# Splitting a 256-query block of the second layer's attention into two blocks of 128

## Chip, cores and metric

The kernel runs on one NeuronCore of a Trainium2 chip. The metric is the device time in microseconds; a median is over the runs named. Before the change: 971.18 us, median of 3 runs (968.93 to 971.66).

## The reference

Two layers, each an attention block and an MLP block, on one sequence of 2048 tokens of width 448. The same weights serve both layers.

```python
x = A_x
for _ in range(2):
    x = x + A(layernorm(x), A_wqkv, A_wo)   # 16 heads of 28, softmax over 2048 keys
    x = x + B(layernorm(x), w1, b1, w2, b2) # relu(x w1 + b1)^2 w2 + b2, F = 1792
```

## The kernel before

Rows are cut into 16 row tiles of 128, numbered 0 to 15. `blocks` says how many tiles form one query block of the attention, for each layer. For every block and every group of four heads (`g`), score matmuls fill a PSUM tile of three banks, one exponential (ScalarE) turns it into bf16, and value matmuls accumulate 28 outputs and one denominator for each head. When all four groups of a block are normalised, the block's **chain** starts: output projection, residual add, layernorm, first MLP product (w1), relu and square, second product (w2), residual add, store.

```python
blocks = [[(0, 4), (4, 4), (8, 4), (12, 4)],
          [(0, 4), (4, 4), (8, 2), (10, 2), (12, 2), (14, 1), (15, 1)]]   # (first tile, tiles)
```

A planner written in the kernel emits the instructions. Each stream is a Python generator with a priority; the planner repeatedly takes the step that can start first by its own table of durations, and PE steps of all streams but the scores are admitted only where, by that table, they delay the next scores or the next exponential by 0.6 us at most. The engines then execute this fixed order, each in its own order.

```python
    pl.spawn(9.5, heat())            # filler matmuls where PE would be too idle
    pl.spawn(0, s_stream())          # scores
    pl.spawn(1, e_stream())          # exponentials
    pl.spawn(2, p_stream())          # values
    ...
            # in norm_stream, once the 4 head groups of a block are normalised:
            pl.spawn(4 + 0.1 * qb, chain(l, qb))
```

```python
    def norm_stream(l, qb, g, res, oe):
        ...
        tail = qb == len(blocks[l]) - 1
        if tail:                     # last block of a layer: denominators by a matmul, no DMA
            def den(e):
                box["t"] = bank(d, "den")
                nc.tensor.matmul(box["t"][:, 0:n], lhsT=sel[:, :], rhs=res["t"][:, 0:n], start=True, stop=True)
            d = Op("PE", 0.1 + n * 4 / 2400, den, deps=[oe], acq=R_m)
            yield d
            ...                      # reciprocal on VectorE
        else:                        # other blocks: three small DMAs around a small reciprocal
            ...

    def chain(l, qb):
        t0, nt = blocks[l][qb]
        ...
        for j in range(nt):
            a = yield from mm_tile(
                [(0, D, [(oTn[:, g, j * P:(j + 1) * P], wo[:, g, :]) for g in range(G)])],
                add_to_x(t0 + j), 0.62, [*norm_done[l, qb], *[("wo", i) for i in range(G)]])
            yield stats(mv, t0, j, [a])
        ...
        xnT, own_xt, ends = yield from layernorm(t0, nt, None, mv=mv)
        own_h = Op("DVE", 0.0, None, acq=R_h)     # one set of 14 h buffers
        yield own_h
        ...                          # w1, relu, square, w2, residual add, store
```

The PSUM banks are dealt out as 2 x 3 for scores, one for the value accumulator, one (`R_m`) for everything else. Once the last scores are planned, the score banks are open to the chains too, and ScalarE takes the relus.

The softmax here doesn't subtract the row's maximum and nothing guards it: scores larger than these inputs give would overflow.

Of the kernel before, what the change touches and what calls it, by code (L numbers as in the profile page):

```python
# [141 lines left out]
def kernel(  # L142
# [18 lines left out]
    NFC = F // P  # L161
    scale = float(DH) ** -0.5

    blocks = [[(0, 4), (4, 4), (8, 4), (12, 4)], [(0, 4), (4, 4), (8, 2), (10, 2), (12, 2), (14, 1), (15, 1)]]

    x_view = A_x[0].rearrange("(tb p) d -> p tb d", p=P)
    out_view = out[0].rearrange("(tb p) d -> p tb d", p=P)
# [37 lines left out]
    part = [[part_sb[:, g, :] for g in range(G)], [k0_f32[:, g * QB:(g + 1) * QB] for g in range(G)]]  # L205
# [360 lines left out]
    def p_stream():  # L566


        where = {}
        for gi, us in enumerate(groups):  # L570
            for k, (pi, kb, r, hh) in enumerate(us):
                where.setdefault((pi, kb), []).append((gi, k, hh))
        steps = list(where.items())
        last_use = {}
        for si, (_, parts) in enumerate(steps):
            for gi, _, _ in parts:
                last_use[gi] = si
        for si, ((pi, kb), parts) in enumerate(steps):
            l, qb, g, kbs, first, last = passes[pi]
            r = 4 // blocks[l][qb][1]  # L580
            n = blocks[l][qb][1] * P
            opens = kb == kbs[0]
            closes = kb + r - 1 == kbs[-1]
            if opens:
                box = {}

            def fn(e, kb=kb, parts=parts, box=box, opens=opens, l=l, g=g, kbs=kbs, r=r, n=n):
                if opens:
                    box["t"] = ps_o.tile([P, QB], DT.float32, name="oT")
                for i in range(r):  # L590
                    for gi, k, hh in parts:
                        c0 = k * 512 + i * n
                        nc.tensor.matmul(box["t"][DHP * hh:DHP * hh + DHP, 0:n],  # L593
                                         lhsT=V_sb[l][:, kb + i, 4 * g + hh, :],
                                         rhs=gbuf[gi]["pt"][:, c0:c0 + n],
                                         start=(kb + i == kbs[0]), stop=(kb + i == kbs[-1]),
                                         tile_position=(0, DHP * hh))
            gis = sorted({p[0] for p in parts})
            o = Op("PE", 0.23 + 0.01 * r, fn,
                   deps=[("e", gis[-1]), *{("V", l, kb + i) for i in range(r)}],  # L600
                   acq=R_o if opens else None,
                   rel=[gbuf[gi]["e"] for gi in gis if last_use[gi] == si], mode="col")
            if opens:
                opened = o
            yield o
            if closes:
                res = {}

                def ev(e, box=box, first=first, last=last, g=g, res=res, n=n, pt=part[qb % 2][g]):
                    src = box["t"][:, 0:n]  # L610
                    if last:
                        dst = res["t"] = np_.tile([P, QB], DT.float32, name="oT_sb")
                        dst = dst[:, 0:n]
                    else:
                        dst = pt
                    if first:
                        nc.vector.tensor_copy(out=dst, in_=src)  # L617
                    else:
                        nc.vector.tensor_tensor(out=dst, in0=src, in1=pt, op=ALU.add)
                oe = Op("DVE", 0.15 + n / 930, ev, deps=[o], rel=opened, acq=R_os if last else None)  # L620
                yield oe
                if last:
                    pl.spawn(3, norm_stream(l, qb, g, res, oe))
# [185 lines left out]
```

## Time and profile before

| | before |
|---|---|
| profiled span | 970.5 us |
| ScalarE busy | 96% |
| last exponential starts | 941.8 us |
| from that start to the end of the span | 28.7 us |

The kernel has two parts that are read differently. Until about 943 us it is a train of 683 exponentials. After it, work that hangs together step by step runs on engines that are mostly idle. In the profiles PE is TensorE, ACT ScalarE and DVE VectorE; PEclk is the clock granted to PE, as a share of full speed. Of the tiles, sc and mt are PSUM banks, den holds denominators, rec their reciprocals, tp transposes, x_sb the residual stream; L417 is the line of the chain's matmuls. The table by 40 slices of the span (24 us each) of the kernel before shows both parts, in tenths busy and tenths of clock:

```profile
ACT  5999999999999999999989999999999999999982
PEclk9999999999999999999979999999999999999998
```

The reader sees ScalarE full from the second slice to the 38th, but for slice 21, and two places where PE's granted clock dips: slices 21 (the boundary of the layers) and 40 (the tail).

### The profile page before, as it was taken

Reading aid. Unit: us, or ns where it says so; the run is one execution under the profiler, and the core shown is the slowest. Engines: PE = TensorE matmul, PEld = TensorE weight load, DVE = VectorE, ACT = ScalarE, POOL = GpSimd, SP = SyncE. Lnnn points to the kernel's source line nnn. Section 1 sums busy time; section 2 is a strip of 40 time slices with the busy share of each in tenths; the row PEclk is TensorE's granted clock in tenths of the full one; section 3 lists DMA queues with packets and bytes.
Section 4 is the critical chain, followed back from the end, with each engine's and each line's share of the span. In section 5 each row is a group of like instructions: output and inputs, shape, how many; then the busy total and the mean of one; then the engine's idle time right before and its main releaser. Section 6 shows DMA issues by size and latency. Waiting matters only on the chain.

```text
span 970.5 us, 18234 instructions
## 1 busy us (share of the span) xinstructions
PE 868.7 (90%) x7764; PEld 318.5 (33%) x7764; DVE 429.5 (44%) x989; ACT 929.9 (96%) x701; POOL 7.5 (1%) x16
## 2 busy tenths in 40 slices
PE   8888899899989998888988999898999899989886
PEld 3233223233222332222323233223233333434555
DVE  7843325434354344553335433325525533343535
ACT  5999999999999999999989999999999999999982
POOL 3000000000000000000000000000000000000000
PEclk9999999999999999999979999999999999999998
DMA  9000010000000000000000000010000000000000
GB/s 272 4 1 1 2 36 12 11 12 13 12 12 4 11 12 13 1 1 1 1 1 1 1 1 1 12 35 24 12 22 20 10 17 27 13 17 23 12 11 14
DMA packets 23005, 17.17 MB, mean 18 GB/s; under 512 B 10634, under 2 KB 19915, under 8 KB 22924
## 3 DMA queue, kind: packets, MB, share of 16 engines
q1 hardware_dynamic: 22924, 16.02, 5.6%
q8 instruction: 60, 0.98, 0.4%
q14 instruction: 21, 0.17, 0.1%
HBM read 13.73 MB, written 2.06 MB: 16 GB/s over the span
## 4 chain that ended last, share of the span: by engine, by line
ACT 64%; issue 17%; PE 14%; DVE 4%; DMA 0%; ACTq 0%
ACT pt L558 64%; PE mt L417 6%; PE sc L543 3%; PE oT L593 3%; PE sc L417 2%; DVE r L719 1%; PE mt L763 1%; DVE rec L641 1%; DVE x_sb L690 0%; DVE st L310 0%; DMA x_sb<-in_A_x_dram 0%; DVE Q_sb L433 0%; DVE xnT L369 0%; PE tp L359 0%; PE den L635 0%
## 5 line engine op out<-in xcount | busy, mean ns | idle before, releaser
L558 ACT ACTIVATE pt<-sc 128x1536 bf16<-128x1536 f32 (+1 forms) x683 | 918.6, 1713 | 10.4 <-PE sc L543 10.1
L543 PE MATMUL sc<-Q_sb,K_sb 32*128 32x512 bf16 (+2 forms) x2816 | 270.0, 324 | 46.7 <-ACT pt L558 38.3
L593 PE MATMUL oT<-pt,V_sb 128*32 128x512 bf16 (+2 forms) x2816 | 206.7, 331 | 0.1
L543 PEld LDWEIGHTS <-K_sb 32*128 32x128 bf16 x2816 | 93.5, 91 | 300.0 <-issue 289.2
L417 PE MATMUL mt<-xnT,w 128*128 128x512 bf16 (+2 forms) x544 | 122.5, 340 | 16.5 <-DVE r L719 11.1
L719 DVE TENSOR_SCALAR r<-mt 128x512 bf16<-128x512 f32 x105 | 72.5, 691 | 129.0 <-PE mt L417 128.8
L417 PE MATMUL mt<-w,h 128*128 128x448 bf16 x420 | 100.3, 357 | 3.0 <-DVE rec L641 1.3
L690 DVE TENSOR_TENSOR x_sb<-x_sb,mt 128x448 bf16<-128x448 bf16 x61 | 37.8, 620 | 132.0 <-PE mt L417 131.4
L593 PEld LDWEIGHTS <-V_sb 128*32 128x32 bf16 x2816 | 58.6, 94 | 113.9 <-issue 110.6
L763 PE MATMUL mt<-xn,ident 128*128 128x448 bf16 x218 | 73.2, 354 | 12.9 <-DVE r L719 2.2
L417 PEld LDWEIGHTS <-w 128*128 128x128 bf16 x616 | 49.6, 101 | 61.0 <-issue 47.0
L417 PEld LDWEIGHTS <-h 128*128 128x128 bf16 x448 | 35.7, 97 | 47.9 <-issue 27.2
L726 DVE TENSOR_TENSOR h<-r 128x512 bf16<-128x512 bf16 (+1 forms) x113 | 47.5, 421 | 7.1 <-ACT r L717 3.9
L417 PE MATMUL mt<-xnT,wq 128*128 128x512 bf16 x124 | 36.5, 381 | 6.0 <-DVE Q_sb L433 3.8
L310 DVE BATCH_NORM_STATS2 st<-x_sb 128x6 f32<-128x448 bf16 x64 | 39.7, 621 | 2.2 <-DMA x_sb<-in_A_x_dram 0.7
L433 DVE CAST Q_sb<-mt 128x512 bf16<-128x512 f32 x30 | 20.7, 689 | 37.3 <-PE mt L417 37.2
L433 DVE CAST K_sb<-mt 128x512 bf16<-128x512 f32 x29 | 20.0, 691 | 36.9 <-PE mt L417 36.9
L459 DVE CAST V_sb<-mt 128x448 bf16<-128x448 f32 x31 | 19.2, 621 | 35.9 <-PE mt L417 35.9
L417 PE MATMUL mt<-xnT,wk 128*128 128x512 bf16 x116 | 31.7, 388 | 2.6 <-DVE K_sb L433 0.9
L417 PE MATMUL mt<-wv,xnT 128*128 128x448 bf16 x124 | 31.4, 375 | 2.7 <-DVE V_sb L459 2.1
L417 PE MATMUL mt<-wo,oTn 128*128 128x448 bf16 x124 | 30.5, 354 | 3.1 <-DVE x_sb L690 1.5
L617 DVE COPY oT_sb<-oT 128x512 f32<-128x512 f32 (+2 forms) x34 | 17.0, 500 | 35.2 <-PE oT L593 34.9
(75 smaller groups left out, 332.7 us busy)
## 6 DMA issues: line engine op xcount, KB each, us to landing
rec<-scr SPq DMA_DIRECT2D x20, 256.0 KB
x_sb<-in_A_x_dram SPq DMA_DIRECT2D x8, 224.0 KB
out_dram<-x_sb SPq DMA_DIRECT2D x16, 112.0 KB
w<-in_B_w_dram SPq DMA_DIRECT2D x1, 1568.0 KB
rec<-scr SPq DMA_DIRECT2D x12, 128.0 KB
w<-in_B_w_dram SPq DMA_DIRECT2D x1, 1344.0 KB
part_sb<-in_A_wqkv_dram SPq DMA_DIRECT2D x1, 672.0 KB
wo<-in_A_wo_dram SPq DMA_DIRECT2D x4, 98.0 KB
```

The source lines that it names most:

```text
L310: nc.vector.bn_stats(out=st[:, :], in_=x_sb[:, t0 + j, :])
L417: nc.tensor.matmul(box["t"][:, c0:c0 + n], lhsT=lhsT, rhs=rhs, start=a, stop=b)
L433: nc.vector.tensor_copy(out=dst, in_=src)
L459: nc.vector.tensor_copy(out=o, in_=i)
L543: nc.tensor.matmul(sc[:, c0:c0 + nt * P], lhsT=K_sb[l][rows, g, (kb + i) * P:(kb + i + 1) * P], rhs=Q_sb[rows, g, t0 * P:(t0 + nt) * P], s ...
L558: nc.scalar.activation(out=pt[:, 0:n], in_=gbuf[gi]["sc"][:, 0:n], func=AF.Exp, scale=scale)
L593: nc.tensor.matmul(box["t"][DHP * hh:DHP * hh + DHP, 0:n], lhsT=V_sb[l][:, kb + i, 4 * g + hh, :], rhs=gbuf[gi]["pt"][:, c0:c0 + n], start ...
L617: nc.vector.tensor_copy(out=dst, in_=src)
L690: nc.vector.tensor_tensor(out=x_sb[:, tb, :], in0=x_sb[:, tb, :], in1=t[:, 0:D], op=ALU.add)
L719: nc.vector.tensor_scalar(out=r[:, 0:w], in0=t[:, 0:w], scalar1=0.0, scalar2=None, op0=ALU.max)
L726: nc.vector.tensor_tensor(out=h[:, 0:w], in0=r[:, 0:w], in1=r[:, 0:w], op=ALU.mult)
L763: nc.tensor.matmul(t[:, 0:D], lhsT=ident[:, :], rhs=xns[0][:, 0:D], start=True, stop=True)
```

## The change

Intent: with tiles 12 and 13 apart, tile 12's chain can start while tile 13's attention still runs, so less chain work should be left at the end.

```diff
-    blocks = [..., [(0, 4), (4, 4), (8, 2), (10, 2), (12, 2), (14, 1), (15, 1)]]
+    blocks = [..., [(0, 4), (4, 4), (8, 2), (10, 2), (12, 1), (13, 1), (14, 1), (15, 1)]]
...
-    def ev(e, ..., pt=part[qb % 2][g]):
+    def ev(e, ..., pt=part[qb % 2][g][:, 0:n]):
```

More of the change, by code (lines that the diff above doesn't have):

```diff
@@ L162 @@
     scale = float(DH) ** -0.5
-    blocks = [[(0, 4), (4, 4), (8, 4), (12, 4)], [(0, 4), (4, 4), (8, 2), (10, 2), (12, 2), (14, 1), (15, 1)]]
+    blocks = [[(0, 4), (4, 4), (8, 4), (12, 4)], [(0, 4), (4, 4), (8, 2), (10, 2), (12, 1), (13, 1), (14, 1), (15, 1)]]
     x_view = A_x[0].rearrange("(tb p) d -> p tb d", p=P)
@@ L607, in p_stream, with ev @@
                 res = {}
-                def ev(e, box=box, first=first, last=last, g=g, res=res, n=n, pt=part[qb % 2][g]):
+                def ev(e, box=box, first=first, last=last, g=g, res=res, n=n, pt=part[qb % 2][g][:, 0:n]):
                     src = box["t"][:, 0:n]
```

## The prediction

> **What bounds the kernel now.** I read the busy table first, then the costliest groups, then the starts of the exponentials stretch by stretch, and last the chain of work that ends the run and the timeline of its last 30 us. The page names the leading engine and the line that loads it:
>
> ```profile
> PE 868.7 (90%) x7764; PEld 318.5 (33%) x7764; DVE 429.5 (44%) x989; ACT 929.9 (96%) x701; POOL 7.5 (1%) x16
> ...
> L558 ACT ACTIVATE pt<-sc 128x1536 bf16<-128x1536 f32 (+1 forms) x683 | 918.6, 1713 | 10.4 <-PE sc L543 10.1
> ```
>
> The 683 softmax exponentials fill ScalarE, which waits only 10.4 us before them in the whole run. PE's 90% is softer: it includes 218 filler matmuls (L763), and PE itself waits 38.3 us for an exponential to free a score buffer. So the attention ends when the last exponential ends, and a block split matters only through the pace of the exponentials, or through what remains afterwards. The pace, from the line of the exponential in three stretches (min/median/max ns, first and last start):
>
> ```profile
> L558 ACT ACTIVATE pt<-sc x45: 1485/1752/1872, 829.1 to 888.0; 128x1536 bf16<-128x1536 f32 x45
> ...
> L558 ACT ACTIVATE pt<-sc x21: 1515/1609/1708, 886.6 to 913.5; 128x1536 bf16<-128x1536 f32 x21
> ...
> L558 ACT ACTIVATE pt<-sc x22: 1182/1758/1849, 913.5 to 941.8; 128x1536 bf16<-128x1536 f32 x21, 128x1024 bf16<-128x1024 f32 x1
> ```
>
> The first stretch is nearly all of block (12, 2), 256 queries wide: 58.9 us over 44 steps, 1.339 us each. The other two are blocks (14, 1) and (15, 1), 128 wide: 26.9/20 = 1.345 and 28.3/21 = 1.348 us. The pitch hardly depends on the width. (Durations exceed the pitch because neighbours overlap.)
>
> The last exponential starts at 941.8 and lasts 1.18, so it ends at 943.0; the span ends at 970.5. These 27.5 us are the tail. The chain of work in it, cut to its long pieces (start, us, what):
>
> ```profile
> 941.63 3.01 PE mt L417 x15
> ...
> 945.34 0.93 PE mt L417 x4
> 946.29 0.63 DVE x_sb L690
> ...
> 952.06 0.59 ACT xnT L367
> 952.69 1.86 PE mt L417 x16
> 954.56 3.04 PE sc L417 x32
> ...
> 958.28 3.00 PE sc L417 x15
> 961.28 0.89 PE mt L417 x16
> ...
> 964.41 2.85 PE sc L417 x15
> 967.28 0.62 DVE x_sb L690
> ```
>
> Read against the order of instructions, this is: the second MLP product (w2) of row tile 13; then the output projection of row tile 14, its layernorm, and its MLP; then the MLP of row tile 15. Two MLPs and a layernorm of about 6 us, nearly bare, stand after the attention. Tile 14's attention was done at about 914, 27 us before the end, but its chain had not even begun: each block's chain takes the one set of h buffers, and the chain of tiles 12 and 13 held it to the end.
>
> [...] the chain's sixteen in 0.89 us are 55.6 ns each, so halving the width costs PE little. [...] the table of 2 us windows (window, length, busy time of PE, weight loads, VectorE, ScalarE, GpSimd, granted clock, DMA):
>
> ```profile
> 950.00:952.00 2.00, 0.96 (x5) 0.62 (x6) 1.52 (x8) 0.00 (x0) 0.00 (x0) 0.56 0.00 0
> 952.00:954.00 2.00, 1.33 (x14) 1.30 (x13) 1.76 (x8) 0.58 (x1) 0.00 (x0) 0.50 0.03 8
> 954.00:956.00 2.00, 2.00 (x22) 2.00 (x20) 1.76 (x10) 0.60 (x1) 0.00 (x0) 0.50 0.00 0
> 956.00:958.00 2.00, 2.00 (x30) 2.00 (x28) 0.50 (x2) 0.96 (x2) 0.00 (x0) 0.73 0.00 0
> ```
>
> A mean of 0.56 means half speed for 1.76 of 2 us, 0.73 for 1.08; with the two full rows 6.84 us[...], after the sparse PE work of 946 to 950.
>
> **The change, part by part.** The edit of the list splits block (12, 2) into (12, 1) and (13, 1). The sliced `part` changes nothing: that view is used only for partial sums, and only blocks of 512 have them.
>
> *Attention of tiles 12 and 13.* The number of exponentials stays 683. Score and value matmuls go from 256 each of 256 columns to 512 each of 128, as the order of instructions shows (128-wide score matmuls 512 to 1024). In the timeline, scores for one exponential cost PE 0.39 us as 6 x 256 and 0.40 us as 12 x 128; one value step 0.40 us as 8 x 256 and 0.41 as 16 x 128. Over some 43 exponentials this is 43 x 0.02 = 0.9 us of PE time, under an engine that is not the bound; the planner also drops 14 fillers (218 to 204). Effect on the end: about 0.
>
> *First MLP product, tiles 12 and 13.* 56 matmuls of 256 columns become 112 of 128: 56 x 0.11 = 6.2 us against 112 x 0.056 = 6.3. Hidden.
>
> *VectorE and DMA.* Four more head groups are copied, inverted and multiplied: 8 x (0.29 + 0.17 + 0.28) - 4 x (0.42 + 0.20 + 0.42) = 1.8 us; one more rsqrt chain of 12 small instructions, about 2.3 us; 12 more small DMAs. VectorE is busy 43% there (11.61 of 27 us). Hidden.
>
> *The tail, where the change acts.* Tile 12's chain can now start one 29 us block earlier. The order of the changed kernel, counted in exponentials, has tile 12's MLP done at 665 of 682, tile 13's w1 at 668 to 676, tile 14's projection already at 677, and 12 of the 15 matmuls of tile 13's w2 before the last scores. After those there remain 3 matmuls of tile 13, then tile 14's transposes and MLP, and all of tile 15's chain. So the projection and layernorm of 14 are hidden, but its MLP is not: the planner still places it after the denominators of tile 15. I lay that order out with the old durations, last exponential ending at 943.0:
>
> - value matmuls end at 943.6 (0.2 wait, 14 of the 32 that took 0.63); copy of the last head group to 943.95; two denominator matmuls end at 944.5.
> - VectorE inverts and multiplies twice: from 944.1, 2 x (0.95 + 0.28) plus gaps, to 946.7. Meanwhile tile 14 is transposed.
> - the last projection matmul and the wait put tile 15's residual add at 947.35 (before: 951.63, 0.65 after the multiply).
> - add to start of normalise took 951.63 to 955.69, 4.06; two h squarings of tile 14 (0.42 each) now stand before it: start 952.25, end 952.65. Tile 14's w1 (56 x 0.056 = 3.1 us plus two fillers) fits between 946.8 and 950.6.
> - tile 15's transposes stand before tile 14's w2 on PE, so w2 starts at 953.0; from w2's start to the next w1 was 958.28 to 961.12, 2.84: 955.85.
> - w1 to the final add was 961.12 to 967.28, 6.16: 962.0. From the add to the end of the span 3.2: 965.2.
>
> That is 5.3 us less than 970.5. [...] Net gain 4.7 us: 971.18 - 4.7 = 966.5.
>
> **Rivals.**
>
> 1. *More matmuls slow the exponentials.* PE gets 512 more matmuls and as many weight loads in 57 us. Against: the blocks of tiles 14 and 15 have this very density and ran at 1.345 and 1.348 us with ScalarE busy 100%. For: their gaps were partly free of chain work, and tile 13's w2 now comes in bursts of six near the end (over 1 us in one interval). A loss of 0.05 us a step would be 2 us: about 968.5.
> 2. *The backlog simply moves.* Two MLPs still lie in the tail, as before. If tile 14's transposes or its w1 wait for something not in my order, such as a late reciprocal DMA or a held PSUM bank, only tile 13's removed w2 matmuls count (12 x 0.19 = 2.3 us): about 969.
> 3. *Tile 14 wholly hidden.* The split's full promise: tile 15 alone after the attention, about 962. The order speaks against it; there are still eight relu steps on ScalarE behind the last exponential.
> 4. [...]
>
> **Range and chances.** The three times before spread over 2.7 us (968.93 to 971.66), and the middle of the run has its own half-clock stretches (489 to 500) whose position may vary. Rivals 1, 2 and 4 push up by 2 to 3 us, rival 3 down by 4. So 966.5, with 963.0 to 970.0 for eight in ten. Two per cent is 19 us, nearly the whole tail, and ScalarE's pitch is untouched: within 2% is nearly sure.
>
> **What would show it.** Right: the last exponential still starts at 941 to 943, pitch 1.34 to 1.35 in all of 829 to 942; four fifths of tile 13's w2 and the projection of 14 before it; from its end to the end of the span about 22 us instead of 27.5; one add of tile 15 near 947 and its layernorm, not tile 14's, as the bare stretch before 953. Wrong: ScalarE idle or a longer pitch after 829 (rival 1); w1 of tile 14 starting later than 949 (rival 2); a granted clock of 0.5 after 953 (rival 4); a tail below 20 us (rival 3).

The sum was 5.3 us for the tail, less 0.6 set aside for the clock, which makes 4.7. The fourth rival, half clock over the final two MLPs, put the time at 968 to 969; it is the "rival 4" named further down.

## The result, and the profile after

Ratios are the mean time of one kernel's fast runs over that of the other's in the same rounds, so they are not quite the ratio of the medians quoted. No run of this document differs from the kernel before by 2%; only the intervals tell them apart.

The changed kernel took 967.09 us (median of 6, 964.36 to 968.28) against 969.35 for the kernel before (6 runs): ratio 0.9971, 95% interval 0.9952 to 0.9991. A repetition gave 965.75 against 969.05, ratio 0.9963 (0.9943 to 0.9984). So the gain is about 3.2 us (the mean of 0.29% and 0.37% of 969), with intervals from 0.9 to 5.5 us, where 4.7 was predicted and 963.0 to 970.0 was the range.

The profiled span fell by much more, from 970.5 to 962.6. That is the first thing to clear up. The busy table and two stretches of the exponential in the changed kernel:

```profile
PE 854.3 (89%) x8267; PEld 327.7 (34%) x8318; DVE 433.4 (45%) x1016; ACT 929.2 (97%) x701; POOL 7.5 (1%) x16
```

```profile
L558 ACT ACTIVATE pt<-sc x45: 1515/1610/1840, 828.2 to 887.2; 128x1536 bf16<-128x1536 f32 x45
...
L558 ACT ACTIVATE pt<-sc x19: 1144/1532/1887, 912.5 to 937.8; 128x1536 bf16<-128x1536 f32 x18, 128x1024 bf16<-128x1024 f32 x1
```

In the first stretch, which the change made 128 wide, the pitch is (887.2 - 828.2)/44 = 1.341 us, against 1.339 before: twice as many matmuls do not slow the exponentials. But the last exponential starts at 937.8 instead of 941.8. Those 4.0 us are not the change's, since they arise before it takes effect at about 825 us: at the 601st exponential (826.91 against 831.74) the changed kernel is already 4.8 us ahead, and from there to the last one it loses 0.9 us. Two stretches around the boundary of the layers show it (columns: stretch, its length, busy us of PE, weight loads, VectorE, ScalarE, GpSimd with counts, granted clock, DMA). The kernel before, first profile:

```profile
440.00:465.00 25.00, 22.36 (x149) 6.96 (x147) 7.79 (x10) 24.02 (x19) 0.00 (x0) 0.93 0.01 1
485.00:520.00 35.00, 31.12 (x189) 9.62 (x187) 12.64 (x16) 31.96 (x25) 0.00 (x0) 0.85 0.00 1
```

The kernel before again, a later profile of the same program:

```profile
440.00:465.00 25.00, 22.37 (x158) 7.25 (x157) 8.06 (x11) 25.00 (x20) 0.00 (x0) 1.00 0.01 1
485.00:520.00 35.00, 30.22 (x208) 9.57 (x208) 15.26 (x21) 34.23 (x26) 0.00 (x0) 0.95 0.00 1
```

In the first, ScalarE stood idle for 0.98 + 3.04 = 4.0 us of these stretches, with PE's mean clock at 0.93 and 0.85; in the second for 0.8 us, at 1.00 and 0.95, and there the last exponential starts at 938.2. The changed kernel's profile happened to be of the second kind (25.00 and 34.22). So two profiles of this kernel are to be compared only after the last exponential:

| profile | last exponential starts | span | from that start to the end |
|---|---|---|---|
| before | 941.8 | 970.5 | 28.7 |
| before, again | 938.2 | 966.9 | 28.7 |
| after | 937.8 | 962.6 | 24.8 |
| after, again | 937.8 | 962.7 | 24.8 |

(The last column, here and below, is taken from the times before rounding.) The tail is 3.9 us shorter, and it repeats to 0.1 us. What took it down, and what was worse than predicted, is in the chain of work of the changed kernel (start, us, what):

```profile
939.43 0.43 PE den L635 x2
...
942.44 0.58 PE tp L359 x4
943.02 3.20 PE sc L417 x20
946.22 0.75 PE mt L763 x2
946.97 1.60 PE sc L417 x16
...
950.41 2.84 PE mt L417 x15
953.25 1.79 PE sc L417 x32
```

Tile 13's w2 and tile 14's projection and layernorm, which stood in this chain before, are gone from it. What follows the last denominators is tile 14's transposes (tp), four projection matmuls of tile 15 with sixteen of w1 (x20), then w2 of tile 14 (x15, on the tile "mt") and w1 of tile 15. But the twenty took 3.20 us; at a clock of 1.00 four such projection matmuls took 0.77 us (*warm2*, its chain below) and sixteen of w1 0.89 (kernel before, at 961.28). Here the granted clock was 0.50 (the kernel before has a stretch of half clock in its tail too, 6.8 us long in both profiles, mostly over w1 of tile 14):

```profile
942.00:944.00 2.00, 1.56 (x8) 0.88 (x8) 0.68 (x2) 0.59 (x1) 0.00 (x0) 0.50 0.00 0
944.00:946.00 2.00, 2.00 (x18) 1.77 (x17) 1.38 (x3) 0.00 (x0) 0.00 (x0) 0.50 0.00 0
946.00:948.00 2.00, 2.00 (x17) 1.55 (x15) 1.63 (x11) 0.60 (x1) 0.00 (x0) 0.50 0.00 0
```

One more loss lies in the attention, where the timeline of the changed kernel has

```profile
917.96 1.89 PE L417 MATMUL mt<-xnT,w 128*128 128x128 bf16 x16
```

```profile
920.50 18.48 ACT L558 ACTIVATE pt<-sc 128x1536 bf16<-128x1536 f32 x14 [0.73 <-PE sc L543]
```

The sixteen matmuls ran at a granted clock of 0.50 (918 to 920; in the same trace sixteen took 1.05 to 1.07 us at 897, 900, 903, 922 and 925) and made the next scores late, and ScalarE stood idle for 0.73 us. The kernel before has no wait of ScalarE for scores between 600 us and its last exponential in either profile. Counted by exponentials, from the 601st to the last, the changed kernel loses 0.87 us against either profile of the kernel before (0.80 in its repetition). So the profiles give -3.9 + 0.9 = -3.0 us, which agrees with the measured 3.2; with intervals of 4 us, so close an agreement is luck.

### The profile page after: what moved, and what is told of

Read it like the earlier page. It is cut to its first block, busy times and chain, and to the rows that moved or that the text cites. A ratio compares the mean times of both kernels' runs of the same rounds, so it can differ in the third digit from the quotient of the medians.

```text
span 962.6 us, 19338 instructions
## 1 busy us (share of the span) xinstructions
PE 854.3 (89%) x8267; PEld 327.7 (34%) x8318; DVE 433.4 (45%) x1016; ACT 929.2 (97%) x701; POOL 7.5 (1%) x16
## 3 DMA queue, kind: packets, MB, share of 16 engines
q8 instruction: 65, 1.06, 0.5%
## 4 chain that ended last, share of the span: by engine, by line
ACT 68%; issue 18%; PE 12%; DVE 1%; ACTq 0%
ACT pt L558 68%; PE mt L417 4%; PE sc L543 3%; PE oT L593 2%; PE sc L417 1%; PE oT L233 1%; PE mt L763 1%; DVE r L719 1%; PE tp L359 0%; DVE xnT L369 0%; DVE rec L641 0%; DVE x_sb L690 0%; PE den L635 0%; ACT r L717 0%; ACT Q_sb L431 0%
## 5 line engine op out<-in xcount | busy, mean ns | idle before, releaser
L543 PEld LDWEIGHTS <-K_sb 32*128 32x128 bf16 x3072 | 98.3, 91 | 298.9 <-issue 287.3
L417 PE MATMUL mt<-xnT,w 128*128 128x512 bf16 (+2 forms) x565 | 116.6, 321 | 16.7 <-DVE r L719 10.7
L417 PE MATMUL mt<-w,h 128*128 128x448 bf16 x434 | 102.9, 355 | 2.5 <-DVE x_sb L690 1.0
L593 PEld LDWEIGHTS <-V_sb 128*32 128x32 bf16 x3072 | 62.6, 94 | 110.2 <-issue 103.9
L763 PE MATMUL mt<-xn,ident 128*128 128x448 bf16 x204 | 68.0, 356 | 9.9 <-DVE xnT L369 1.5
L417 PEld LDWEIGHTS <-h 128*128 128x128 bf16 x448 | 35.2, 97 | 45.4 <-issue 23.9
L726 DVE TENSOR_TENSOR h<-r 128x512 bf16<-128x512 bf16 x114 | 47.5, 418 | 5.6 <-ACT r L717 2.5
L417 PE MATMUL mt<-xnT,wq 128*128 128x512 bf16 x115 | 34.5, 380 | 7.2 <-DVE Q_sb L433 4.1
L417 PE MATMUL mt<-xnT,wk 128*128 128x512 bf16 x103 | 30.2, 381 | 3.4 <-DVE K_sb L433 0.9
L369 DVE COPY xnT<-tp 128x1024 bf16<-128x1024 bf16 (+1 forms) x31 | 20.8, 672 | 27.2 <-PE tp L359 27.2
```

The source lines that it names most:

```text
L369: nc.vector.tensor_copy(out=dst, in_=tp[:, :, 0:w])
L417: nc.tensor.matmul(box["t"][:, c0:c0 + n], lhsT=lhsT, rhs=rhs, start=a, stop=b)
L543: nc.tensor.matmul(sc[:, c0:c0 + nt * P], lhsT=K_sb[l][rows, g, (kb + i) * P:(kb + i + 1) * P], rhs=Q_sb[rows, g, t0 * P:(t0 + nt) * P], s ...
L593: nc.tensor.matmul(box["t"][DHP * hh:DHP * hh + DHP, 0:n], lhsT=V_sb[l][:, kb + i, 4 * g + hh, :], rhs=gbuf[gi]["pt"][:, c0:c0 + n], start ...
L726: nc.vector.tensor_tensor(out=h[:, 0:w], in0=r[:, 0:w], in1=r[:, 0:w], op=ALU.mult)
L763: nc.tensor.matmul(t[:, 0:D], lhsT=ident[:, :], rhs=xns[0][:, 0:D], start=True, stop=True)
```

## The experiments

All were compared with the kernel before in the same rounds (6 runs each, 11 of the kernel before; 5 for *late_after*), and all gave the right result but for *warm* and *warm_before*. "Tail" is, as in the table above, from the start of the last exponential to the end of the span; the expectations of the first eight runs count it from the end of that exponential, which is 1.05 to 1.33 us later, so both are given. The expectations work with rounded times and can differ from the table by 0.1.

| run | ratio (95% interval) | last exp. starts | tail from its start / end |
|---|---|---|---|
| before_again | 0.9995 (0.9975 to 1.0016) | 938.2 | 28.7 / 27.5 |
| after_again | 0.9963 (0.9943 to 0.9984) | 937.8 | 24.8 / 23.7 |
| attn_only | 0.9974 (0.9956 to 0.9992) | 942.6 | 24.2 / 23.2 |
| chain_only | 0.9995 (0.9974 to 1.0017) | 937.4 | 27.6 / 26.3 |
| split10 | 1.0028 (1.0009 to 1.0047) | 940.2 | 30.2 / 29.0 |
| late_after | 0.9996 (0.9979 to 1.0013) | 938.7 | 27.8 / 26.6 |
| prio_before | 0.9938 (0.9920 to 0.9956) | 937.6 | 23.8 / 22.4 |
| warm | 0.9977 (0.9961 to 0.9992) | 941.5 | 25.1 / 24.0 |
| warm_before | 1.0026 (1.0008 to 1.0044) | 940.1 | 30.4 / 29.2 |
| warm2 | 0.9947 (0.9929 to 0.9965) | 938.9 | 23.2 / 22.0 |
| den_free | 0.9978 (0.9960 to 0.9996) | 942.4 | 25.0 / 23.9 |
| best | 0.9931 (0.9915 to 0.9948) | 940.9 | 23.5 / 22.1 |

### Noise: both kernels again

*after_again*, no edit.

> The changed kernel unaltered. In the first pair of profiles the tail (end of the last exponential to end of the span) went from 27.5 to 23.6 us, and the last exponential started 4.0 us earlier (941.8 to 937.8). Theory: only the tail belongs to the change, so the time falls by about 3.9 us (ratio 0.996), and a new profile has a tail of 22 to 24.5 us and its last exponential anywhere in 937 to 943. Rival: the earlier exponentials belong to the change too; then the time falls by about 8 us (ratio 0.992) and the last exponential starts near 938 again.

*before_again*, no edit.

> The kernel before unaltered, for the noise and a second profile of its tail. Ten profiles so far put the start of the last exponential at 937.4 to 942.6 whatever the kernel, near 937.5 where ScalarE waited 6 us in all for scores and near 942 where it waited 9 to 11. Theory (that spread is the clock's, not the kernel's): ratio 1.000 within 0.002, last exponential anywhere in 937 to 943, and from its start to the end of the span 27 to 29.5 us (28.7 in the first profile). Rival: the old kernel's attention really ends later, again near 942.

Both theories held against their rivals: the last exponential of all fourteen profiles falls anywhere from 937.4 to 942.6, and the kernel before reaches 938.2 too. Only the tail belongs to the kernel. The six times of *after_again* show the two kinds of run: 963.8 to 964.4 three times, 967.1 to 967.9 three times.

### Which half of the change does it?

*attn_only*: attention split, one chain for tiles 12 and 13 together.

```diff
+        ck = (l, 4) if l == 1 and qb == 5 else (l, qb)      # tile 13 joins tile 12's chain
+        off = P if ck != (l, qb) else 0
...
-        if len(norm_done[l, qb]) == G:
-            pl.spawn(4 + 0.1 * qb, chain(l, qb))
+        if len(norm_done[ck]) == (2 * G if ck == (1, 4) else G):
+            pl.spawn(4 + 0.1 * ck[1], chain(*ck))
```

> Attention of tiles 12 and 13 in two blocks of 128, but one chain (projection, layernorm, MLP) for both together, as before. By its order, tile 14's projection and layernorm are done before the last scores, all 15 matmuls of tile 13's w2 remain behind them. Theory (the tail holds what the order leaves there): last value matmuls about 1.6 us later than in the changed kernel, so a tail near 25.2 us and a time about 2.3 us under before. Rival 1 (twice the attention matmuls slow the exponentials): pitch above 1.36 us after 829 and a time above before. Rival 2 (only the finer chains matter): same as before.

Measured: ratio 0.9974, 2.5 us under before, and a tail of 23.2 us from the end of the last exponential, 2 us shorter than expected, even a little shorter than the whole change's 23.6. Its clock was 1.00 in every 2 us window of the tail up to 966. Rivals 1 and 2 are out. Its attention again lost time at half clock: ScalarE waited 1.24 us for scores at 935.87, behind six w2 matmuls that took 2.42 us (granted clock 0.53 from 934 to 936; in the changed kernel six took 1.31 us at 936.10, at 1.00).

*chain_only*: attention in one block of 256, a chain for each tile.

```diff
+            if (l, qb) == (1, 4):
+                pl.spawn(4 + 0.1 * qb, chain(l, qb, 0))
+                pl.spawn(4 + 0.1 * qb + 0.05, chain(l, qb, 1))
```

> Attention of tiles 12 and 13 in one block of 256 as before, but a chain for each of them. By its order 8 of tile 13's w1 and all of its w2 remain behind the last scores, tile 14's projection and layernorm do not; w2 of 13 stands after the last denominator, so it fills PE's idle time. Theory: a tail of 24 to 25 us, about 3 us under before. Rival (the finer attention blocks are what counts): same as before within 0.5 us.

A miss: no gain in time, and a tail of 26.3 us. The order of its tail is as read, but PE ran at half clock twice in it. Two windows and the w2 of tile 14 in its chain of work (3.0 us in the kernel before, 2.84 after):

```profile
938.00:940.00 2.00, 2.00 (x38) 1.31 (x30) 1.47 (x10) 1.13 (x2) 0.00 (x0) 0.53 0.00 0
952.00:954.00 2.00, 2.00 (x7) 0.88 (x6) 0.00 (x0) 0.00 (x0) 0.00 (x0) 0.50 0.00 0
```

```profile
951.30 4.52 PE mt L417 x15
```

So the two halves cannot be added up: each edit gives the planner another order, and with it the half clock another place (0.50 from 942 to 948 in the changed kernel; here 0.53 from 938 to 940 and 0.50 from 952 to 954). The 1.5 us more of this w2 would cover most of the distance to the expected 24 to 25 us; no run took the half clock away here.

*split10*: the same splitting one block earlier.

```diff
-    (8, 2), (10, 2), (12, 1), (13, 1), (14, 1), (15, 1)
+    (8, 2), (10, 1), (11, 1), (12, 2), (14, 1), (15, 1)
```

> The same amount of splitting one block earlier: (10, 2) into (10, 1) and (11, 1), (12, 2) left whole. By its order both projections, the layernorm of 14 and both MLPs stay behind the last scores; only 10 of tile 13's 15 w2 matmuls move ahead. Theory: it gains only those, about 2 us (ratio 0.998), tail 25 to 26 us. Rival (more and finer blocks give slack everywhere, wherever the split is): as much as the changed kernel, 3 to 4 us.

A miss for both: it is slower than before by 0.28%, tail 29.0 us. The rival that finer blocks help anywhere is refuted. The theory had the direction wrong. The trace suggests why, though no run tests it: both projections were planned behind both last denominators, so the layernorms of tiles 14 and 15 ran one after the other on VectorE with PE idle:

```profile
946.00:948.00 2.00, 0.91 (x5) 0.20 (x2) 1.90 (x6) 0.00 (x0) 0.00 (x0) 1.00 0.00 0
948.00:950.00 2.00, 0.00 (x0) 0.00 (x0) 1.65 (x12) 0.00 (x0) 0.00 (x0) 1.00 0.00 0
950.00:952.00 2.00, 0.61 (x4) 0.45 (x5) 1.79 (x10) 0.19 (x1) 0.00 (x0) 0.62 0.00 0
```

PE (first figure after the length) does nothing for two microseconds, VectorE is nearly full, and the half clock follows: 0.62 from 950 to 952, 0.50 from 952 to 956.

### Is it the split, or what stands behind the last exponential?

Two runs and the two kernels make a square. *prio_before* has no split at all; only tile 14's chain takes precedence over that of tiles 12 and 13:

```diff
-            pl.spawn(4 + 0.1 * qb, chain(l, qb))
+            pl.spawn(4 + 0.1 * (3.5 if (l, qb) == (1, 5) else qb), chain(l, qb))
```

> The kernel before with no split: only tile 14's chain is given precedence over the chain of tiles 12 and 13. By its order tile 14's projection and layernorm then come before the last scores and about 23 w2 matmuls of tiles 12 and 13 stay behind them, beside the denominators. Theory (what counts is which latency-bound work is behind the last exponential, not the block size): tail 23.5 to 25 us, 3 us or more under before, the clock at 1.0 for longer. Rival (the finer blocks themselves count): same as before.

*late_after* has the split, but tile 14's projection waits for the last scores, so its layernorm is behind them again:

```diff
+            *([("s", len(groups) - 1)] if (l, qb) == (1, 6) else [])   # in chain's first deps
```

> The changed kernel, split kept, but tile 14's projection is made to depend on the last scores, so that it and the layernorm lie behind them as in the kernel before. With the kernel before, the changed one and the precedence run this makes a square: split or not, tile 14's layernorm early or late. Theory (early or late decides): start of the last exponential to the end 26.5 to 28 us, time only 1 to 2 us under before. Rival (the split itself shortens the tail): about 24.8 us and 3.6 us under before, as the changed kernel.

| tail from the start of the last exponential, us | layernorm of 14 behind the last scores | before them |
|---|---|---|
| no split | 28.7 and 28.7 (before) | 23.8 (prio_before) |
| split | 27.8 (late_after) | 24.8 and 24.8 (after) |

The column decides, the row does not: 3 to 5 us from left to right, 1 us from top to bottom, with either sign. In time, *late_after* is the same as before (0.9996), *prio_before* is 6.0 us faster (0.62% of 969.6), nearly twice the change's gain, without one added matmul. Two limits. *chain_only* stands between the columns: its residual add of tile 14 starts before the last scores (935.11 against 936.53), but the normalisation only at 942.04, and its tail is 27.6. And the half clock goes along with the columns: PE ran at half clock for 6.8 us of the tail in the kernel before, 10.2 in *late_after*, 6.8 in the changed kernel, 0 in *prio_before*. As an estimate, it cost the kernel before about 2 us (w1 of tile 14 took 5.6 us from 952.69 on, some transposes included, that of tile 15 3.3 from 961.12 on); that leaves about 3 us between 28.7 and 23.8 to the order itself. No correct run has the kernel before at full clock. The chains of work show the two. *late_after*:

```profile
940.79 0.93 PE mt L417 x4
941.75 0.64 DVE x_sb L690
...
948.15 1.86 PE mt L417 x16
```

From the residual add of tile 14 to its w1 there are 6.4 us, filled by VectorE's layernorm and one reciprocal, with PE idle for about half of it and at half clock from about 943 (0.76 from 942 to 944, 0.50 from 944 to 952). *prio_before*, timeline of the same place:

```profile
939.62 1.68 PE L417 MATMUL sc<-w,h 128*128 128x448 bf16 x8
...
941.35 1.30 PE L417 MATMUL sc<-w,h 128*128 128x448 bf16 x6
...
943.62 1.06 PE L417 MATMUL sc<-xnT,w 128*128 128x128 bf16 x16
```

Here the w2 matmuls of tiles 12 and 13, which nobody waits for, fill PE while VectorE inverts tile 15's denominators, and tile 14's w1 follows at once. The clock stays at 1.00 from 936 to 962. The "3 us or more" expected came out as 6.0.

### The half clock of the tail

*warm*: six filler matmuls after each of the last two denominator matmuls, in unused columns of their bank.

```diff
+                for _ in range(6 if g >= 2 else 0):
+                    nc.tensor.matmul(box["t"][:, P:QB], lhsT=ident[:, :], rhs=xns[1][:, 0:QB - P], start=True, stop=True)
```

> The changed kernel with six filler matmuls of 384 columns after each of the last two denominator matmuls, into unused columns of the same PSUM bank, so that PE stays busy while VectorE inverts. In the changed kernel's profile the granted clock was 0.5 from about 941.7 to 948.1, and the last residual add came 1.2 us later than predicted. Theory (the half clock cost this): granted clock 1.0 through the tail, tail about 1.2 us shorter than the changed kernel's, near 22.4, time about 5 us under before. Rival (VectorE's serial inversions and the single denominator bank set the add): clock restored but tail the same within 0.4 us.

*warm_before*: the same in the kernel before, sixteen after the last one.

```diff
+                for _ in range(16 if g >= 3 else 0):
+                    nc.tensor.matmul(box["t"][:, P:QB], lhsT=ident[:, :], rhs=xns[1][:, 0:QB - P], start=True, stop=True)
```

> The kernel before with sixteen filler matmuls of 384 columns (2.6 us) after the last denominator matmul. Before had half clock for 6.84 us in its tail, and its 56 matmuls of w1 of tile 14 took 5.6 us instead of about 3.5. Theory (half clock is part of the old tail's length): clock at 1.0, tail about 2 us shorter, near 25.5. Rival (VectorE's layernorm and inversions set the tail): no change within 0.5 us.

Both gave a **wrong result**, by a mistake in the edit: the same function serves the last block of layer 0, whose denominators fill all 512 columns, and the fillers overwrote them. Both are inconclusive in time for another reason, which the chain of *warm* shows (L637 is the fillers, L643 the reciprocal):

```profile
943.50 0.99 PE den L637 x6
...
944.51 0.97 DVE rec L643
```

The reciprocal waited for the fillers, about 1 us each time, which gave back what the clock gained (1.00 in every 2 us window from 936 to 964, where the changed kernel had 0.50 from 942 to 948). In *warm_before* the sixteen fillers (2.61 us in its chain) lay on the path in the same way, and the half clock came all the same: 0.50 from 954 to 956, 0.66 from 956 to 958. The "about 3.5" of its expectation was the author's estimate; w1 of tile 15, at 1.00 in the kernel before, took 3.3 us.

*warm2*: mended, with a score bank of their own and in the last tile only.

```diff
+            if l == 1 and g >= 2:
+                def fill(e):
+                    t = bank(j, "mt")
+                    for _ in range(6):
+                        nc.tensor.matmul(t[:, 0:384], lhsT=ident[:, :], rhs=xns[1][:, 0:384], start=True, stop=True)
+                j = Op("PE", 0.95, fill, deps=[d], acq=R_sc)
+                yield j
+                yield Op("PE", 0.0, None, deps=[j], rel=j)
```

> The filler test again, mended: in the first one the fillers stood between the denominator matmul and its signal, so each reciprocal waited 1.0 us for them, and the same code ran at the end of layer 0 too, where it overwrote the denominators (hence the wrong result). Now the fillers have a score bank of their own and only the last tile has them; the order of everything else is that of the changed kernel. From the start of the last exponential to the end of the span the changed kernel took 24.8 and 24.9 us. Theory (half clock delayed the last projection and tile 14's w1): clock 1.0, residual add 1.2 us earlier, about 23.2 us. Rival (VectorE alone sets it): 24.5 to 25.

Measured: tail 23.2 us from the start, as expected, result correct, ratio 0.9947 (against 0.9971 and 0.9963 of the changed kernel, with overlapping intervals: the time alone does not show the difference). Windows of the same stretch, and the chain:

```profile
942.00:944.00 2.00, 1.93 (x14) 1.22 (x15) 1.42 (x3) 0.14 (x1) 0.00 (x0) 1.00 0.02 4
944.00:946.00 2.00, 2.00 (x27) 1.52 (x25) 1.31 (x3) 0.86 (x2) 0.00 (x0) 1.00 0.00 0
```

```profile
943.44 0.38 PE tp L359 x4
943.82 0.77 PE sc L417 x4
944.62 0.63 DVE x_sb L698
```

The residual add of tile 15 stands 5.8 us after the start of the last exponential (944.62 - 938.86), in the changed kernel 6.7 (944.55 - 937.84). The other part lies between this add and w2 of tile 14. The changed kernel's timeline:

```profile
944.55 0.62 DVE L690 TENSOR_TENSOR x_sb<-x_sb,sc 128x448 bf16<-128x448 bf16 x1 [1.84 <-PE sc L417]
...
950.24 2.81 PE L417 MATMUL mt<-w,h 128*128 128x448 bf16 x14
```

*warm2*:

```profile
944.62 0.62 DVE L698 TENSOR_TENSOR x_sb<-x_sb,sc 128x448 bf16<-128x448 bf16 x1 [0.90 <-PE sc L417]
...
949.70 2.81 PE L417 MATMUL mt<-w,h 128*128 128x448 bf16 x14
```

That is 5.7 us against 5.1: in the changed kernel a squaring of tile 14 that the planner put before tile 15's normalisation had to wait for w1 at half clock. From w2 to the end both take 12.3 us. With twelve useless matmuls the tail lost 0.95 + 0.6 = 1.6 us: the half clock (0.50 from 942 to 948, here 1.00) cost the changed kernel that much.

*den_free*: the other suspect for the late add, the one bank of the denominators.

```diff
-            d = Op("PE", 0.1 + n * 4 / 2400, den, deps=[oe], acq=R_m)
+            d = Op("PE", 0.1 + n * 4 / 2400, den, deps=[oe], acq=pools_now())
```

> The changed kernel with the denominators of the last tile allowed in any free PSUM bank instead of one bank alone. In the changed kernel the last denominator matmul waited 1.05 us for the reciprocal of the one before, and the transposes of tile 14 another 1.05 us. Theory (those waits lie beside VectorE's two inversions, which run one after the other anyway): tail 0 to 0.5 us shorter. Rival (the bank is the cause of the missing 1.2 us): tail 1 to 1.5 us shorter.

Tail 25.0, unchanged, as the theory said; ratio 0.9978. The two reciprocals run back to back now, but the planner used the time to place sixteen w1 matmuls of tile 14, at half clock (0.61 from 946 to 948, 0.54 from 948 to 950), ahead of the projection of 15. So this run shows that the bank alone gains nothing here, not that the wait was free in every order.

### A version that beats both

*best*: *prio_before*, with *den_free*'s edit, and the reciprocal square root of tile 15 planned in four pieces, so that squarings of tile 14 can go between.

```diff
-        rs = Op("DVE", 2.3, rsqrt, deps=[last])
-        yield rs
+        if tail:                                     # tile 15 of layer 1
+            rs = Op("DVE", 0.58, rsqrt0, deps=[last])
+            yield rs
+            for _ in range(3):
+                rs = Op("DVE", 0.58, newton, deps=[rs])
+                yield rs
```

> The kernel before without a split, tile 14's chain first (23.7 us from the start of the last exponential to the end), and two changes more: the last denominators in any free bank, so that the second reciprocal need not wait 0.7 us for the first, and the reciprocal square root of tile 15 in four pieces, so that tile 14's h squarings can stand between them and w2 starts about 0.9 us earlier. Expected 22.0 to 22.5 us, time about 7.5 us under before (ratio 0.992). If the tail is bound otherwise (by PE's own 2 x 6 us of MLP), it stays at 23.5 and the ratio at 0.994.

Ratio 0.9931, 963.58 us, faster than both kernels, but not better than *prio_before* beyond the noise: its tail is 23.5 us, not 22. In its chain

```profile
943.67 2.46 PE sc L433 x13
```

the leftover w2 matmuls of tile 13 now stand all together between the last denominator and the projection of tile 15, so PE took the place of the reciprocal. The simplest good version is therefore *prio_before*, one changed priority.

One idea needed no run. The kernel before planned with one set of h buffers of their own for the single tiles gives the same steps in the same order. Planned with a set for each single tile, nothing changes before the w1 of tile 15, at the very end. The h buffers do not hold back tile 14.

## Why the prediction was right or wrong

The range held and "within 2%" was right; the size was 4.7 us against 3.2 measured. By its steps:

1. *ScalarE's pitch is untouched by width.* Right: 1.341 us against 1.339.
2. *Rival 1, a slower attention.* Put at 2 us; it came true at 0.8 to 0.9 us, but at half clock, when sixteen matmuls took 1.89 us, and not by the pitch. PE was busy for 1.06 of the 2 us from 914 to 916; the granted clock was 0.89 from 916 to 918 and 0.50 from 918 to 920. That the missing fillers (204 instead of 218; the last before the tail at 882.6 us instead of 928.0) left this stretch sparse and so brought the half clock is the author's guess; no run tests it. The prediction counted their loss as without effect.
3. *The tail's order as read.* Right: 3 matmuls of tile 13 after the last scores, then tile 14's MLP, then tile 15's.
4. *The sum of the tail, 5.3 us without clock losses.* Right within 0.2: *warm2*, the same order at full clock, has a tail 5.5 us shorter than before (28.7 - 23.2). In part this is luck: the layout had the add 0.3 us too early after the last exponential's end (4.35 us; *warm2* 4.6) and the way from there to w2 0.6 us too long (5.65; *warm2* 5.1).
5. *The clock's allowance, 0.6 us.* This is the term that was mis-sized. It was the allowance for half clock over w2 of 14 or w1 of 15, set against a cost that no trace showed. The half clock came earlier, over the projection of tile 15 and w1 of tile 14 (0.50 from 942 to 948), and cost 1.6 us. The step that failed is the residual add of tile 15: in the predicted layout 4.35 us after the last exponential's end (947.35 - 943.0), measured 5.6 (944.55 - 938.98). VectorE was done on time (its second multiply ended at 942.71, 3.7 us after the exponential, as laid out); the projection on PE then took 1.84 us until the add instead of 0.65. The later steps kept their predicted length (add to w2 5.7 us against 5.65, w2 to w1 2.84, w1 to the last add 6.2), but the first of them only because the half clock lengthened it from the 5.1 of *warm2*. The second denominator's wait for its bank, which the layout also missed (it had both by 944.5), lay beside the reciprocals: *den_free* gained nothing. In sum: 5.5 - 1.6 of the clock in the tail - 0.9 in the attention = 3.0 us, where the prediction had 5.3 - 0.6 = 4.7.
6. *Why tile 14's chain was late before.* Wrong. The prediction said that the h buffers held it. In the code above the chain takes h buffers only after its layernorm, so they cannot delay the projection; planning with more of them moves neither, and *prio_before* shows that precedence in the planner alone brings both forward. Nor could the chain start at 914: the multiply of tile 14's last head group ran only at 928.06 in the kernel before, 924.47 in the changed one.
7. *What the split is for.* The prediction took the split as the cause. The square of runs shows it as only one way to another order: with the split and tile 14 late the gain in time is gone, without the split and with tile 14 early it is nearly twice as large.
8. *Matmuls of 128 columns.* The prediction read 55.6 ns each from sixteen in 0.89 us. Right: 32 of w1 in a row took 1.79 us in the chain of the changed kernel, 55.9 ns each.

What stays open is why the planner lets tile 14's projection in after the split and not before it. The order shows it slipping in between the w1 and w2 steps of the chain ahead; which of the planner's comparisons tipped was not tried.

## What to carry to other kernels

Where one engine's train bounds a kernel and a dependent tail follows, ask what must stand behind the last item of the train, and put the steps that only wait (inversions, layernorm) before or beside throughput work that nobody waits for; try the precedence before the tiling. An edit of sizes under a planner is an edit of the order, so test the order by itself. In two tails idle time of PE was followed by half clock: in *split10* PE was busy for 0.00 of the 2 us from 948 to 950, and the clock was 0.62, then 0.50 up to 956; in the changed kernel it was busy for 0.49 of the 2 us from 940 to 942, and the clock was 0.50 from 942 to 948. Not every such stretch was: in *warm* PE was busy for 0.95 and 0.98 us in the two windows from 944 to 948, and the clock stayed at 1.00. Fillers helped where nobody waited for their signal (*warm2*, tail 23.2 us against 24.8), not where each reciprocal waited about 1 us for them (*warm*, 25.1).
